# One score round moved behind the first MLP layer, and the words around it reordered, in a fused attention and MLP kernel

## The chip, the cores and the metric

The kernel runs on one core of one Trainium2 chip. The metric is the device time of one launch in microseconds (us); each kernel is timed in several runs and the median is compared. Five engines work side by side, each through its own instructions in order: TensorE (PE in the profile; its weight loads have a row of their own, PEld), VectorE (DVE), ScalarE (ACT), GpSimd (POOL) and SyncE (SP). SP and POOL also issue the DMA transfers. They wait for each other only through semaphores.

## The reference

Attention with a forget gate, followed by an MLP with a tanh GELU, over 8 batches of 576 tokens, 8 heads of 64 and a model width of 512. Cut to what matters:

```python
scores = scale * q @ k.T                                   # per batch and head, 576 x 576
cum = cumsum(log(clip(f, 1e-4, 1)))
scores = where(causal, -1e9, scores + cum[:, None] - cum[None, :])
attn = softmax(scores)
x = (attn @ v)            # -> (4608 tokens, 512)
h = x @ w_in              # 512 -> 2048
out = gelu_tanh(h) @ w_out  # 2048 -> 512
```

## The kernel before

The work is written out as a list of short words in tables (FRONT, SECOND, STEADY, FLUSH, LAST, lines 71 to 112). `run` (line 845) walks a table and emits the instructions of each word in that order; nothing is rescheduled afterwards, so the order of words is the order of instructions on every engine. FRONT covers everything up to the last pieces of chunk 1's second layer.

Attention is done by quads, a quad being four heads of one batch: quads 2 and 3 make batch 1, quads 4 and 5 batch 2, quad 6 begins batch 3. The MLP is done by chunks of 512 tokens. The words that matter here:

- `S.i.r` is score round r of quad i, `H.i.r.g` the same round for two of its four heads (`scores`, line 268). Matrix products of 32 rows, one for each head side by side, go into two PSUM tiles `ps_s` of two heads each (pool `psS`, two buffers); then ACT takes the exponential of each tile into `pt` (line 294), which frees the tile. A round of four heads takes both buffers, a half round one.
- `M.i.r` sets the entries above the diagonal to zero on POOL (line 300), `m.i.r` does it on DVE by a product with a triangle (line 330).
- `D.i` is the denominator product, one PSUM tile `po` and three DVE instructions (line 365); `V.i.x` and `v.i.x` are the two halves of the product with the values and their DVE division into `xT` (line 383). `v` uses a `psS` buffer in place of `po`.
- `VW.i` (POOL) and `vw.i` (DVE) weight the values into `vw` (line 234); `CL.i` (DVE) and `cl.i` (ACT) then copy one block of `vw` to other partitions (line 239). Two buffers each of `pt`, `vw`, `qT`, `kT`, `q_c`, `k_c` and `v_nat` alternate.
- `I.c.p` is one of eight pairs of the first layer of chunk c: eight products of 512 columns into a `psS` buffer, then a GELU on ACT (line 412).
- `F.c.n` and `f.c.n` emit n steps of the second layer of chunk c, in one matrix product of 128 columns of weights (`F`) or in four of 32 columns side by side (`f`). Chunk 0 has 64 steps (`mlp_out`, line 682), chunk 1 has 112 (`seven_products`, line 606).
- `J` is the first layer of chunk 0. `U`, `UW`, `PW` and `G` are sums of weights and of GELU results for the seven-product schemes, on DVE or POOL.
- `LK.i`, `LQ.i` load k and q of a quad from POOL's queue; `LV.b.half` loads four heads of v from SP's queue in five transfers; `LC` loads v from POOL's queue. `TK.i`, `TQ.i` transpose k and q on DVE.
- `X` and `Y` are one-element activations that touch the exponential and the GELU. ACT keeps the table of one of the two at a time; where the next function is of the other kind a table load stands before it.

Three places of the order matter for the steps below. In FRONT before, quad 4's round 0 is done in two halves, `H.4.0.0 H.4.0.1`, between `D.3` and `V.3.1`, ahead of the eight `I.1` words; `cl.4` stands behind all eight of them; and POOL issues `LK.5 LQ.6 LK.6` in a row, ahead of the masks `M.3.2` and of `VW.4`. `VW.4` reads the half of `v_nat` that `LV.2.0` loads.

Of the kernel before, what the change touches and what calls it, by code (L numbers as in the profile page):

```python
# [16 lines left out]
def kernel(  # L17
# [12 lines left out]
    B, H, S, D = q.shape  # L30
# [44 lines left out]
        H.1.0.0 B.1.128 B.1.512 B.1.128 B.1.512 M.1.0 B.1.128 V.0.1.0 H.1.2.0 H.0.1.1 V.0.0.0 H.0.3.0 D.1.0 V.1.1.0 j.0.0.4 M.0.1 UT LQ.2  # L75
        WI.7 V.1.0.0 H.0.3.1 H.1.3.1 j.0.0.4 j.0.0.8 H.1.1.0 vw.0.1 WI.6 H.1.1.1 RJ.0.0 M.0.3 D.0.1 LK.2 WO.1 WO.0 j.0.1.8 VW.1.1 H.1.2.1
        H.1.3.0 M.1.3 V.0.1.1 V.0.0.1 J.0.2 j.0.1.8 M.1.1 D.1.1 tr V.1.0.1 V.1.1.1 GJ.0.1 W.1 TQ.2 J.0.3 J.1.1 GJ.0.0 J.1.3 J.1.0 U.0 WO.2
        J.1.2 LK.3 WO.3 LQ.3 LC.1.0 PW.2.1 PW.2.2 F.0.3 LC.1.3 f.0.2 LC.1.4 LC.1.1 LC.1.2 TK.2 LQ.4 f.0.2 S.2.0 F.0.5 TK.3 m.2.0 F.0.4 LK.4
        F.0.1 S.2.2 F.0.2 f.0.5 TQ.3 f.0.2 S.2.1 f.0.3 LV.2.1 F.0.6 S.3.0 F.0.2 m.2.1 vw.2 cl.2 F.0.2 f.0.1 LV.2.0 X M.2.2 D.2 M.3.0 LQ.5
        f.0.1 S.3.1 VW.3 f.0.2 V.2.0 LK.5 TQ.4 TK.4 f.0.4 S.3.2 LV.3.1 LQ.6 f.0.1 m.3.1 f.0.3 LK.6 V.2.1 M.3.2 f.0.4 S.4.1 F.0.5 VW.4 TQ.5  # L80
        F.0.1 X H.4.2.0 H.4.2.1 D.3 f.0.1 cl.3 H.4.0.0 H.4.0.1 V.3.1 v.3.0 vw.5 U.1 f.0.2 m.4.2.2 I.1.2 I.1.1 UW.2.4 TK.6 I.1.0 CL.5 U.2
        m.4.2.3 I.1.3 I.1.5 TQ.6 U.3 TK.5 I.1.4 G.0 I.1.6 M.4.1 I.1.7 F.1.1 G.1.1.2 cl.4 F.1.5 LV.3.0 F.1.5 S.5.0 F.1.5 M.5.0 F.1.7 m.4.0
        F.1.2 UW.2.3 F.1.2 LK.8 F.1.7 LK.7 D.4 S.5.1 F.1.17 LQ.8 F.1.1 S.5.2 M.5.2.3 M.5.2.2 f.1.2 V.4.0 f.1.1 M.5.1 f.1.8 LQ.7@m.3.1 f.1.1
        V.4.1 S.6.0 M.6.0 f.1.4 D.5 f.1.10 S.6.1 f.1.1 M.6.1 f.1.2 V.5.1 vw.6 F.1.4 CL.6 F.1.5 S.6.2 m.6.2.3 V.5.0 f.1.4 m.6.2.2 f.1.3
    """

    SECOND = """
# [35 lines left out]
    def many(n, shape, dtype, name):  # L123
        return [singles.tile(shape, dtype, name=f"{name}{i}") for i in range(n)]
# [11 lines left out]
    vw = many(2, [128, NT + 1, 4, D], BF16, "vw")  # L136
# [760 lines left out]
```

## Time and profile before

| | |
|---|---|
| median of 3 runs | 320.56 us (320.35 to 320.78) |
| the profiled execution's own time | 320.43 us |
| its span, first to last instruction | 318.7 us |
| granted TensorE clock | 1.00 |
| first step of chunk 0's second layer starts | 38.4 us |
| quad 4's round 0 starts | 61.2 us |
| chunk 1's first layer | 64.3 to 78.1 us |
| chunk 2's first layer starts (FRONT is done) | 99.1 us |

All that the change touches lies between 38.4 and 99.1 us. The chain of waits names, in order of time, the work that the end hung on. A timeline lists the instructions of one engine with start and duration; what stands in brackets is the idle time before and who ended it. In both, "x24" counts instructions that are shown as one piece; some matmul records are missing, so the counts of matmuls can be a little low. In the chain a piece of matmuls lasts until the next piece starts.

### The profile page before, as it was taken

To read this page: it belongs to the slowest core of one execution; us is meant where nothing else is said; L and a number is where in the kernel's file an instruction comes from. 1 tells how busy PE (TensorE), PEld (TensorE's weight loads), DVE (VectorE), ACT (ScalarE), POOL (GpSimd) and SP (SyncE) were. 2 spreads that over 40 slices of the span, in tenths; PEclk is the share of its full clock that TensorE was granted. 3 is DMA by queue.
4 is the path that set the end of the run, shared out by engine and by line. 5 is a ranking of instruction groups with operands and counts; after the bars stand their busy time and mean duration, and the time that the engine had idled before them with its cause. 6 is when DMAs were issued, how large, how long until landed. Compare 5 with 4: busy or idle time off the path is not lost.

```text
span 318.7 us, 11738 instructions
## 1 busy us (share of the span) xinstructions
PE 313.0 (98%) x5290; PEld 220.3 (69%) x5309; DVE 246.0 (77%) x368; ACT 212.9 (67%) x248; POOL 109.6 (34%) x146
## 2 busy tenths in 40 slices
PE   8999999999999999999999999999999999999996
PEld 3468744545776577776788878767776786688785
DVE  7775638699978879879877987699876865597674
ACT  3676777866766876877777866787596744836610
POOL 8789525250340417311850075205610140000000
PEclk9999999999999999999999999999999999999999
DMA  7999998933364901593139411961011111010213
GB/s 126 239 203 199 209 227 190 233 106 75 70 117 127 193 6 39 129 199 72 39 80 232 89 39 37 217 147 38 5 39 62 35 37 35 30 38 2 99 35 100
DMA packets 47491, 33.41 MB, mean 105 GB/s; under 512 B 29777, under 2 KB 42193, under 8 KB 47441
## 3 DMA queue, kind: packets, MB, share of 16 engines
q0 software_dynamic: 9632, 15.99, 28.1%
q1 hardware_dynamic: 37664, 16.60, 19.4%
q8 instruction: 41, 0.67, 0.9%
q14 instruction: 10, 0.07, 0.1%
q10 hardware_dynamic: 144, 0.07, 0.1%
HBM read 36.85 MB, written 9.44 MB: 145 GB/s over the span
## 4 chain that ended last, share of the span: by engine, by line
PE 97%; issue 1%; DVE 0%; ACT 0%
PE ps_w L620 31%; PE ps_h L404 19%; PE ps_s L286 10%; PE ps_q L540 10%; PE po L356 9%; PE ps_h L440 5%; PE pso L693 4%; PE ps_u L488 4%; PE idle_ps L259 3%; PE po_m L342 2%; PE idle_ps L265 1%; PE ps_p L620 1%; PE ps_o L356 0%; ACT pt L294 0%; DVE xT L388 0%
## 5 line engine op out<-in xcount | busy, mean ns | idle before, releaser
L294 ACT ACTIVATE pt<-ps_s 128x1024 bf16<-128x1024 f32 (+2 forms) x100 | 93.9, 991 | 36.6 <-PE ps_s L286 34.9
L300 POOL TENSOR_SCALAR_AFFINE_SELECT pt<-pt 128x512 bf16<-128x512 bf16 (+3 forms) x70 | 44.3, 645 | 99.1 <-ACT pt L294 76.3
L404 PE MATMUL ps_h<-xT,w_in_sb 128*128 128x512 bf16 (+1 forms) x307 | 65.5, 357 | 0.8 <-issue 0.2
L404 PEld LDWEIGHTS <-w_in_sb 128*128 128x128 bf16 x320 | 31.1, 98 | 26.4 <-issue 0.6
L412 ACT ACTIVATE gT<-ps_h 128x1024 bf16<-128x1024 f32 x34 | 34.6, 1017 | 20.3 <-PE ps_h L404 20.1
L620 PEld LDWEIGHTS <-gT 128*32 128x32 bf16 (+1 forms) x1177 | 43.9, 97 | 5.7 <-issue 2.2
L620 PE MATMUL ps_w<-w_out_sb,gT 128*32 128x256 bf16 (+1 forms) x996 | 42.7, 273 | 0.0
L620 PEld LDWEIGHTS <-gsum 128*32 128x32 bf16 (+1 forms) x909 | 35.1, 97 | 3.9 <-issue 1.7
L286 PE MATMUL ps_s<-qT,kT 32*128 32x64 bf16 (+5 forms) x896 | 35.1, 261 | 0.1
L556 DVE TENSOR_TENSOR usnap<-ps_q,usnap 128x1024 f32<-128x1024 f32 x15 | 17.9, 1221 | 17.3 <-PE ps_q L540 12.7
L234 POOL TENSOR_TENSOR vw<-v_nat,wT 128x1280 bf16<-128x1280 f32 (+1 forms) x12 | 27.9, 2326 | 7.6 <-DMA v_nat<-in_v_dram 7.3
L620 PE MATMUL ps_w<-usum,gsum 128*32 128x256 bf16 (+1 forms) x752 | 29.8, 273 | 0.0
L286 PEld LDWEIGHTS <-kT 32*128 32x128 bf16 x896 | 16.1, 92 | 16.5 <-issue 10.8
L637 DVE COPY snap<-ps_w 128x512 f32<-128x512 f32 x32 | 21.8, 682 | 6.5 <-PE ps_w L620 6.3
L551 ACT ACTIVATE gT<-usnap 128x1024 bf16<-128x1024 f32 x15 | 15.8, 1053 | 11.0 <-DVE usnap L556 10.7
L388 DVE TENSOR_TENSOR xT<-po,rb 128x576 bf16<-128x576 f32 x26 | 19.5, 751 | 4.3 <-PE po L356 3.9
L356 PE MATMUL po<-pt,vw 128*32 128x64 bf16 (+4 forms) x624 | 22.4, 278 | 0.0
L217 DVE STREAM_TRANSPOSE kT<-k_c 128x576 f32<-128x576 f32 x16 | 19.4, 1244 | 2.5 <-DMA k_c<-in_k_dram 2.5
L356 PEld LDWEIGHTS <-vw 128*32 128x32 bf16 x672 | 14.6, 97 | 9.3 <-issue 2.6
L217 DVE STREAM_TRANSPOSE qT<-q_c 128x576 f32<-128x576 f32 x16 | 19.8, 1249 | 0.4 <-DMA q_c<-in_q_dram 0.3
L210 POOL DMA_DIRECT2D k_c<-in_k_dram x16 | 9.1, 570 | 30.0 <-DVE kT L217 17.4
L540 PEld LDWEIGHTS <-w_in_sb 128*128 128x128 bf16 x160 | 15.7, 98 | 2.1
(135 smaller groups left out, 491.7 us busy)
## 6 DMA issues: line engine op xcount, KB each, us to landing
out_dram<-o_st SPq DMA_DIRECT2D x35, 256.0 KB, 2.2
k_c<-in_k_dram POOLq DMA_DIRECT2D x16, 288.0 KB, 5.4
q_c<-in_q_dram POOLq DMA_DIRECT2D x16, 288.0 KB, 6.3
v_nat<-in_v_dram SPq DMA_DIRECT2D x16, 256.0 KB, 5.0
v_nat<-in_v_dram SPq DMA_DIRECT2D x20, 128.0 KB, 5.1
v_nat<-in_v_dram POOLq DMA_DIRECT2D x8, 256.0 KB, 9.6
w_in_sb<-in_moe_w_in_dram POOLq DMA_DIRECT2D x8, 256.0 KB, 8.5
w_out_sb<-in_moe_w_out_dram POOLq DMA_DIRECT2D x4, 512.0 KB, 11.3
```

Source lines behind the costliest of these rows:

```text
L217: return nc.vector.transpose(out=dst.rearrange("p s c -> p (s c)").bitcast(FP32) .rearrange("p (t a) -> p a t", a=n), in_=src.rearrange("p ...
L234: return eng.tensor_mul(vw[i % 2][:, t0:t1], vb[:, t0:t1, h0:h0 + 4, :], wT[:, i, t0:t1, :].unsqueeze(3).to_broadcast([128, t1 - t0, 4, D]))
L286: nc.tensor.matmul(tiles[h // 2][:, h % 2, c0:c0 + nq], key_columns(i, key, h, c), qq[32 * h:32 * h + 32, q0:q0 + nq, c], start=(c == 0 an ...
L294: nc.scalar.activation(p[:, 2 * g:2 * g + 2, off:off + n], t[:, :, 0:n], AF.Exp, scale=scale)
L300: nc.gpsimd.affine_select(out=x, in_=x, compare_op=ALU.is_ge, fill=0.0, base=0, pattern=pattern, channel_multiplier=-1)
L356: nc.tensor.matmul(po[r0:r0 + w.shape[-1], 448 + q0:448 + q0 + nq], w, p[:, h, col:col + nq], start=(key in (0, "low")), stop=(key in ("lo ...
L388: nc.vector.tensor_mul(xT[:, 2 * u + x, r0 + s0:r0 + s1], po, rbs[i, part])
L404: nc.tensor.matmul(ph[:, j, n * cols:(n + 1) * cols], w_in_sb[:, dt, 128 * ft:128 * ft + 128], xT[:, dt, h0:h0 + cols], start=(dt == 0 and ...
L412: nc.scalar.activation(gelus(c, 2 * pr, 2), ph, AF.Gelu_apprx_tanh)
L540: nc.tensor.matmul(ps[:, k, HC * n:HC * n + HC], w[:, d, 128 * n:128 * n + 128], x[:, d, :], start=(first and n == 0 and d == 0), stop=(d ...
L620: nc.tensor.matmul(ps[c0:c0 + width, n, cols[0]:cols[1]], x[:, j, 128 * n + c0:128 * n + c0 + width], w[:, j, cols[0]:cols[1]], start=(fir ...
L637: copy(kept[name], ps)
```

## The change

The tail of FRONT is rewritten, from the second layer of chunk 0 on. Other tables and all functions are as before.

```diff
-        J.1.2 LK.3 WO.3 LQ.3 LC.1.0 PW.2.1 PW.2.2 F.0.3 LC.1.3 f.0.2 LC.1.4 LC.1.1 LC.1.2 TK.2 LQ.4 f.0.2 S.2.0 F.0.5 TK.3 m.2.0 F.0.4 LK.4
-        F.0.1 S.2.2 F.0.2 f.0.5 TQ.3 f.0.2 S.2.1 f.0.3 LV.2.1 F.0.6 S.3.0 F.0.2 m.2.1 vw.2 cl.2 F.0.2 f.0.1 LV.2.0 X M.2.2 D.2 M.3.0 LQ.5
-        f.0.1 S.3.1 VW.3 f.0.2 V.2.0 LK.5 TQ.4 TK.4 f.0.4 S.3.2 LV.3.1 LQ.6 f.0.1 m.3.1 f.0.3 LK.6 V.2.1 M.3.2 f.0.4 S.4.1 F.0.5 VW.4 TQ.5
-        F.0.1 X H.4.2.0 H.4.2.1 D.3 f.0.1 cl.3 H.4.0.0 H.4.0.1 V.3.1 v.3.0 vw.5 U.1 f.0.2 m.4.2.2 I.1.2 I.1.1 UW.2.4 TK.6 I.1.0 CL.5 U.2
-        m.4.2.3 I.1.3 I.1.5 TQ.6 U.3 TK.5 I.1.4 G.0 I.1.6 M.4.1 I.1.7 F.1.1 G.1.1.2 cl.4 F.1.5 LV.3.0 F.1.5 S.5.0 F.1.5 M.5.0 F.1.7 m.4.0
-        F.1.2 UW.2.3 F.1.2 LK.8 F.1.7 LK.7 D.4 S.5.1 F.1.17 LQ.8 F.1.1 S.5.2 M.5.2.3 M.5.2.2 f.1.2 V.4.0 f.1.1 M.5.1 f.1.8 LQ.7@m.3.1 f.1.1
-        V.4.1 S.6.0 M.6.0 f.1.4 D.5 f.1.10 S.6.1 f.1.1 M.6.1 f.1.2 V.5.1 vw.6 F.1.4 CL.6 F.1.5 S.6.2 m.6.2.3 V.5.0 f.1.4 m.6.2.2 f.1.3
+        LK.3 WO.3 J.1.2 F.0.1 LQ.3 F.0.1 LC.1.0 PW.2.1 PW.2.2 F.0.3 LC.1.3 LC.1.4 LC.1.1 LC.1.2 TK.2 F.0.2 LK.4 S.2.0 LQ.4 F.0.5 TK.3 m.2.0
+        F.0.4 S.2.2 F.0.10 S.2.1 TQ.3 X F.0.3 LV.2.1 F.0.6 S.3.0 f.0.4 m.2.1 vw.2 cl.2 f.0.2 LV.2.0 M.2.2 D.2 M.3.0 LQ.5 S.3.1 VW.3 LV.3.1
+        f.0.4 LK.5 V.2.0 f.0.3 S.3.2 TK.4 f.0.2 TQ.4 V.2.1 M.3.2 m.3.1 f.0.5 S.4.1 LQ.6 f.0.2 LK.6 f.0.1 UW.2.4 f.0.2 D.3 f.0.1 VW.4 X cl.3
+        H.4.2.1 H.4.2.0 V.3.1 f.0.1 v.3.0 cl.4 F.0.2 I.1.7 I.1.0 TQ.5 TK.5 vw.5 cl.5 I.1.1 TK.6 TQ.6 I.1.2 I.1.5 U.1 I.1.4 I.1.3 U.2 F.1.1
+        m.4.2.2 I.1.6 LV.3.0 m.4.2.3 G.0 G.1.1.2 F.1.6 U.3 m.4.1 F.1.4 S.4.0 F.1.6 LK.8 F.1.6 m.4.0 F.1.2 S.5.0 M.5.0 PW.2.3 LK.7 D.4 f.1.9
+        S.5.1 F.1.12 LQ.8 F.1.6 S.5.2 M.5.2.2 M.5.2.3 V.4.0 f.1.2 m.5.1 f.1.4 f.1.5 V.4.1 S.6.0 M.6.0 f.1.6 D.5 f.1.6 S.6.1 M.6.1 f.1.5
+        V.5.1 f.1.5 vw.6 f.1.2 S.6.2 CL.6 m.6.2.3 f.1.4 M.6.2.2 V.5.0 LQ.7 f.1.6
```

What is other in kind, not only in place: `H.4.0.0 H.4.0.1` become `S.4.0`, behind the first layer and eleven second-layer steps of chunk 1; `CL.5` becomes `cl.5` (DVE to ACT); `M.4.1` and `M.5.1` become `m.4.1` and `m.5.1` (POOL to DVE), `m.6.2.2` becomes `M.6.2.2` (DVE to POOL), `UW.2.3` becomes `PW.2.3` (DVE to POOL). The steps of the second layers are the same in number, 64 of chunk 0 and 97 of chunk 1, divided otherwise between `F` and `f`: 31 and 33 of chunk 0 become 37 and 27, 61 and 36 of chunk 1 become 43 and 54. The extra dependency `@m.3.1` of `LQ.7` is gone. On ACT `cl.4` now stands ahead of the first GELU's table load, and POOL issues `LQ.6` and `LK.6` behind the two masks of `M.3.2`. SP's order of transfers is the same.

## The prediction, made before the changed kernel ran

> **What bounds the kernel.** I read the page's busy shares and the summary of the chain first.
>
> ```profile
> PE 313.0 (98%) x5290; PEld 220.3 (69%) x5309; DVE 246.0 (77%) x368; ACT 212.9 (67%) x248; POOL 109.6 (34%) x146
> PE 97%; issue 1%; DVE 0%; ACT 0%
> ```
>
> TensorE is busy 98% of the span and carries 97% of the chain. A change of order gains only by making TensorE's own stream cheaper, and loses whatever it lets TensorE wait. So I took the chain in order of time, from chunk 0's second layer to FRONT's end, for the price of each kind of piece:
>
> ```profile
> 42.91 0.57 PE ps_s L286 x14
> ...
> 60.21 0.80 PE po L356 x24
> 61.01 0.21 PE pso L693 x4
> 61.23 1.01 PE ps_s L286 x17
> ...
> 78.30 1.20 PE ps_w L620 x11
> 79.50 0.62 PE ps_s L286 x24
> 80.12 2.62 PE ps_w L620 x23
> 82.74 0.79 PE po L356 x24
> ...
> 87.08 0.68 PE po L356 x24
> 87.77 1.09 PE ps_w L620 x40
> ...
> 99.14 0.21 PE ps_h L404
> ```
>
> Eleven `F` steps of chunk 1 take 1.20 us (78.30), ten `f` steps, which are 40 products, 1.09 us (87.77): 0.109 us a step either way; a step of chunk 0 is 0.21 us (61.01). So `F` for `f` changes nothing in itself. But 23 `F` steps behind a score round take 2.62 us, where 23 x 0.109 is 2.51, and a product `po` behind `F` steps takes 0.79 (82.74), behind `f` steps 0.68 (87.08). Whenever TensorE changes between the three tilings (score rows; 128 columns: `F`, `I`, `J`; 32 columns: `f`, `D`, `V`) it loses 0.11 us, except on entering a score round: 11 steps and then scores (78.30) show no extra.
>
> **What the change gains.** Counting those changes of tiling in the two word lists, from the first step of chunk 0's second layer to the end of FRONT, I find 23 before and 17 after; 14 and 9 of them lie ahead of the `I.1` words. Six fewer: -0.66 us. Quad 4's round 0 in two halves takes 1.01 us (61.23), a whole round 0 takes 0.62 (79.50): -0.39. Two pieces of TensorE's timeline, the two halves of `H.4.2` and the eight `I.1` words:
>
> ```profile
> 58.84 1.38 PE L286 MATMUL ps_s<-qT,kT 32*128 32x320 bf16 x16
> ...
> 64.25 14.04 PE L404 MATMUL ps_h<-xT,w_in_sb 128*128 128x512 bf16 x62
> ```
>
> The halves start at 58.84 and `D.3` follows at 60.21, where two rounds of 0.57 (42.91) would be 1.14: about 0.25 is waiting, for the second exponential of `S.4.1` (57.60 + 1.94 in ACT's timeline below). After the change `D.3` stands between `S.4.1` and `H.4.2`, so that wait goes: -0.25. In sum -1.30 us.
>
> **What it loses on ACT and PSUM.** A round's tiles come free only with its exponentials, so the next whole round cannot finish its start before them. ACT's timeline:
>
> ```profile
> 40.76 1.94 ACT L294 ACTIVATE pt<-ps_s 128x1024 bf16<-128x1024 f32 x2
> ...
> 54.45 1.94 ACT L294 ACTIVATE pt<-ps_s 128x1024 bf16<-128x1024 f32 x2 [0.72 <-PE ps_s L286]
> ...
> 57.60 1.94 ACT L294 ACTIVATE pt<-ps_s 128x1024 bf16<-128x1024 f32 x2 [1.21 <-PE ps_s L286]
> ...
> 78.33 1.02 ACT L412 ACTIVATE gT<-ps_h 128x1024 bf16<-128x1024 f32 x1 [0.70 <-PE ps_h L404]
> 79.38 0.40 ACT L239 COPY vw<-vw 64x256 bf16<-64x256 bf16 x1
> 79.80 1.28 ACT L294 ACT_TABLE_LOAD   x1
> 81.10 1.94 ACT L294 ACTIVATE pt<-ps_s 128x1024 bf16<-128x1024 f32 x2
> ```
>
> Let T be the end of the last `I` (78.30 before). Before, the exponentials of `S.5.0` start late, at 81.10, behind GELU, copy and table load, but 23 steps and `D.4` stand before `S.5.1`, and that hides it. After: the GELU ends at T+1.05, with `cl.4` gone the load at T+2.35, the exponentials of `S.4.0` at T+4.31. TensorE needs ten steps (1.09), `S.4.0` (0.62), then 14 steps and a change of tiling (1.64): it is at `S.5.0` at T+3.35, and the heads of the second tile wait until T+4.35. That is +1.0 us. `S.5.1` follows behind `D.4` (0.79) and nine `f` steps (0.98), 1.77 us, where the exponentials of `S.5.0` need 1.94 and some 0.08 of handing over: +0.25. Later pairs of rounds have 2.0 us or more between them (18 `F` steps and a change of tiling are 2.07): nothing. At the front, `S.2.2` now comes after nine steps and no `f`, at about 42.6 instead of 42.91, while the exponentials of `S.2.0` still end at 42.70: +0.15. In sum +1.4 us; from below 1.0, if the two small ones are hidden, to 1.9, if `D.4` also waits. It waits for the mask `m.4.0`, now the last of a queue on DVE:
>
> ```profile
> 74.64 1.21 DVE L587 TENSOR_TENSOR w_out_sb<-w_out_sb 128x2048 bf16<-128x2048 bf16 x1
> ...
> 80.22 0.69 DVE L600 TENSOR_TENSOR gsum<-gsum,gT 128x1024 bf16<-128x1024 bf16 x1
> 80.83 0.68 DVE L637 COPY snap<-ps_w 128x512 f32<-128x512 f32 x1
> 81.43 0.41 DVE L330 TENSOR_TENSOR pt<-pt,causal 128x512 bf16<-128x512 bf16 x1
> ```
>
> From the GELU's end at T+1.1 on, two such sums (1.38), `U.3` (1.21), `m.4.1` (0.41), the copy (0.68) and `m.4.0` (0.41): T+5.2 without overlap, about T+5.0 with the tenth or so by which neighbours overlap in these rows; `S.5.0` ends at T+4.97. I take nothing for it.
>
> The Trainium skill (ScalarE: Activation LUTs, What ACT_TABLE_LOAD costs) speaks harder against the change: it states 1.28 us for the load and as much as 1.38 us of draining with every switch. The rows agree with the first and show no second: copy, load and exponential follow within 0.02 us. By the page's 2.66 us the wait at `S.5.0` alone would be 1.4 us longer.
>
> **What it loses behind `cl.4`.** `cl.4` copies what `VW.4` writes. Before, it stood behind all GELUs, and nobody noticed that `VW.4` ran late. Now table load and all GELUs of chunk 1 queue behind it, and TensorE waits for them with the third `I`, which needs the PSUM buffer of the first. POOL, SP and the transfers:
>
> ```profile
> 52.80 2.33 POOL L234 TENSOR_TENSOR vw<-v_nat,wT 128x1280 bf16<-128x1280 f32 x1
> 55.09 0.59 POOL L210 DMA_DIRECT2D k_c<-in_k_dram  x1
> 55.68 0.54 POOL L210 DMA_DIRECT2D q_c<-in_q_dram  x1
> 56.34 0.53 POOL L210 DMA_DIRECT2D k_c<-in_k_dram  x1
> 56.88 1.24 POOL L300 TENSOR_SCALAR_AFFINE_SELECT pt<-pt 128x512 bf16<-128x512 bf16 x2
> 65.39 2.90 POOL L234 TENSOR_TENSOR vw<-v_nat,wT 128x1280 bf16<-128x1280 f32 x1 [7.27 <-DMA v_nat<-in_v_dram]
> ```
>
> ```profile
> 55.06 2.37 SPq L187 DMA_DIRECT2D v_nat<-in_v_dram  x1
> ```
>
> ```profile
> k_c<-in_k_dram POOLq DMA_DIRECT2D x1, 288.0 KB, 6.7
> q_c<-in_q_dram POOLq DMA_DIRECT2D x1, 288.0 KB, 7.7
> k_c<-in_k_dram POOLq DMA_DIRECT2D x1, 288.0 KB, 8.7
> v_nat<-in_v_dram SPq DMA_DIRECT2D x1, 128.0 KB, 5.9
> v_nat<-in_v_dram SPq DMA_DIRECT2D x1, 64.0 KB, 10.2
> ```
>
> Added to their issue times, `LK.5` lands at 61.8, `LQ.6` at 63.4, `LK.6` at 65.0, and the last fifth of `LV.2.0`, whose issue took SP from 55.06 to 57.43, at 65.3; its neighbour one place ahead needed only 5.9. `VW.4` starts at 65.39 with that landing. The queue of v went almost silent while POOL's ran: the queue tables of the microseconds from 56 and from 60 have
>
> ```profile
> q1 hardware_dynamic: 941, 0.24, 105.4%
> ...
> q1 hardware_dynamic: 29, 0.01, 4.3%
> ```
>
> q1 being SP's queue. I read it as service in the order of arrival: the v piece came in behind all three loads of k and q.
>
> After the change the `I` words start at 64.25 less five changes of tiling (0.55), the moved round (1.01) and the wait (0.25), plus 0.15: 62.6. An `I` lasts 1.73 (eight products of 0.216, the 0.21 of a chunk 0 step), so the third starts at 66.05. Ahead of it ACT must do copy 0.40, load 1.28 and GELU 1.02, with hand-overs 2.8: `VW.4` must end by 63.25, and start by 60.9 at 2.33 us or 60.35 at 2.90. POOL now issues `LQ.6` and `LK.6` behind `M.3.2`, whose exponentials end at 56.39 before (54.45 + 1.94) and within 0.1 of that after: masks until 57.6, loads issued 57.6 and 58.2, just behind SP's 57.43. In order of arrival the v piece then waits only for `LK.5` (61.8) and lands 0.3 later (as 65.3 to 65.0): 62.1. `VW.4` ends 64.4 to 65.0, the GELU frees the buffer 67.2 to 67.8: +1.2 to +1.75, I take +1.5. Bounds: with its neighbour's 5.9 it lands at 61.0: +0.1; if nothing helps it, 65.3: +4.4 to +5.0. I take the value between since one of three loads stays ahead of it. It cannot be a gain.
>
> The other moved words I put at nothing. `cl.5` on ACT (0.40) falls into the 0.70 us that ACT idles before each GELU (78.33), and costs up to 0.4 there if `vw.5` is late; the masks moved to DVE have until `D.4` and `D.5`, and each costs its 0.41 if it is not ready; `PW.2.3` has POOL's idle time and until chunk 2 uses it; `LK.4` and `LQ.4` change places on POOL's queue, and the chain's summary, with 0% of DVE, shows nothing that waits for a transpose; `LQ.7` loses a gate, far from its use, and `LK.8` and `LK.7` stay behind the `I` words.
>
> **Sum.** -1.3 + 1.4 + 1.5 = +1.6 us on the profiled execution's 320.43: 322.0. The median is 0.13 above that execution, so 322.1 us.
>
> **Rivals.**
>
> *The load keeps its old place* (chance 0.20). A load issued only 0.2 us behind SP's last piece can still be served ahead of it, and then the v piece lands at 65.3: -1.3 + 1.4 + 4.7, 325.4 us. For it: the piece was slow although SP began to issue it at 55.06, ahead of `LK.5`; against it: its neighbour was not.
>
> *No wait behind `cl.4`* (0.22). The piece lands by 61, the gain and the waits on PSUM cancel: 320.7 us. For it, the 5.9 us of the neighbour; against it, `LK.5` landing at 61.8 on the same engines. The Trainium skill (DMA: Bandwidth & Descriptors, Queues, rings and completion order) states that each DMA engine takes turns between its queues packet by packet, and by that rule the time would be this one. The trace does not agree: 941 packets a microsecond against 29 are no turns at that scale.
>
> *Faster* (0.08). No wait behind `cl.4`, and `S.5.0` waits little, as the heads of the first tile run ahead: -1.3 + 0.3, 319.6 us. Against it: the products of the four heads are issued in turn, so the first of the second tile holds up the rest; it decides for this case only if the exponentials end by T+3.7.
>
> **Chances and range.** Forecast 0.50, the rivals 0.20, 0.22, 0.08. Within 0.2% (0.64 us, what a measurement of this kernel can tell from no change) is the third case; slower are the forecast and the first, 0.70. Low 320.2 and high 325.8 leave out the last case and the far sides of the first and third, 0.18 in all; the forecast's own range is 321.4 to 322.9.
>
> **What would show it.** Right: on ACT `cl.4` idle for POOL's `VW.4`, the first GELU of chunk 1 starting about 66 where TensorE finished its pair at 64.3, a hole of 1 to 2 us on TensorE in the third `I`, and another of 1 us at `S.5.0` behind a table load; `VW.4` starting near 62. Wrong: `VW.4` done by 63.2 with no hole in the `I` words; FRONT ending before 98.5; or a hole elsewhere, as at `D.4` or `D.3`.

## The result: slower by 0.56%

| | before | after |
|---|---|---|
| median | 320.53 us (8 runs, 320.35 to 322.08) | 322.50 us (8 runs, 321.51 to 323.15) |
| profiled execution | 320.43 us, span 318.7 | 321.97 us, span 320.0 |
| ratio of the times | | 1.0056, 95% interval 1.0044 to 1.0068 |

The loss is 1.97 us. The runs of after spread over 1.6 us, and its profiled execution is one of the faster ones: it shows 1.5 of the 2.0 us. Of these 1.5 the spans account for 1.3; time less span is 1.81 to 1.97 us in the eight runs of after and 1.7 in the kernel before, and no view shows what takes the 0.2 between them. One run among the experiments, 328.11 us in e6_early_loads, is more than 1.5% above the fastest of its kernel and is left out of the medians. Page of the profile after:

```profile
span 320.0 us, 11820 instructions
...
PE 314.0 (98%) x5345; PEld 221.3 (69%) x5345; DVE 244.1 (76%) x367; ACT 213.1 (67%) x249; POOL 108.5 (34%) x146
...
q8 instruction: 42, 0.69, 0.9%
...
PE 94%; ACT 2%; DVE 1%; DMA 1%; issue 0%
```

TensorE is still the bound, but ACT now has 2% of the chain, where before it had none. The chain of waits of after, in order of time:

```profile
42.63 0.81 PE ps_s L286 x10
...
62.65 12.14 PE ps_h L404 x56
...
76.67 1.02 ACT gT L412
77.71 1.28 ACT L294
79.00 1.95 ACT pt L294 x2
80.99 0.73 PE ps_s L286 x21
81.72 1.93 ACT pt L294 x2
83.69 0.63 PE ps_s L286 x14
...
99.58 1.73 PE ps_h L404 x8
```

From 76.67 on the chain runs through ACT: last GELU, table load, the exponentials of `S.4.0`, and only then the rest of `S.5.0`; one round later the exponentials of `S.5.0` hold up `S.5.1`. TensorE's timeline gives the sizes:

```profile
62.49 12.30 PE L404 MATMUL ps_h<-xT,w_in_sb 128*128 128x512 bf16 x56
...
80.08 0.20 PE L286 MATMUL ps_s<-qT,kT 32*128 32x64 bf16 x2
80.99 0.69 PE L286 MATMUL ps_s<-qT,kT 32*128 32x64 bf16 x22 [0.71 <-ACT pt L294]
81.61 0.87 PE L356 MATMUL po<-pt,w_bf 128*32 128x512 bf16 x24
...
83.39 0.94 PE L286 MATMUL ps_s<-qT,kT 32*128 32x64 bf16 x16
84.26 1.70 PE L620 MATMUL ps_w<-usum,gsum 128*128 128x256 bf16 x14
```

A timeline's duration runs a little into the next piece, so a round is best timed from its start to the start of what follows. `S.5.0` starts at 80.08 and `D.4` follows at 81.61: 1.53 us for a round 0, which takes 0.62 without waiting, so 0.91 us of waiting. `S.5.1` takes 0.87 (83.39 to 84.26) where 0.57 is usual, 0.30 too much; `S.2.2` takes 0.81 in the chain, 0.24 too much. The `I` words start at 62.49, where 64.25 stood before, and run through without a hole. Why there is none stands in the rows of POOL and ACT:

```profile
60.64 2.33 POOL L234 TENSOR_TENSOR vw<-v_nat,wT 128x1280 bf16<-128x1280 f32 x1 [1.54 <-DMA v_nat<-in_v_dram]
```

```profile
63.00 0.40 ACT L239 COPY vw<-vw 64x256 bf16<-64x256 bf16 x1 [0.89 <-POOL vw L234]
63.42 1.28 ACT L412 ACT_TABLE_LOAD   x1
64.72 1.02 ACT L412 ACTIVATE gT<-ps_h 128x1024 bf16<-128x1024 f32 x1
```

ACT does wait for `VW.4`, as predicted, but in this execution the v piece landed at 60.6. The first GELU ends at 65.74, and the third `I` is due at 62.49 + 2 x 1.73 = 65.95: 0.2 us to spare. FRONT ends at 99.58 against 99.14. The other 0.9 us of the span lie behind it: 0.6 in the last 4 us. DVE's last piece and the span's end are 2.89 us apart before (315.81 and 318.7), and 3.51 after:

```profile
316.49 0.29 DVE L660 TENSOR_TENSOR v_nat<-ps_p,snap 128x128 f32<-128x128 f32 x1 [0.15 <-PE ps_p L620]
```

### The profile page after: what moved, and what is told of

It is laid out like the page before. It is cut to its first block, busy times and chain, and to the rows that moved or that the text cites. A ratio compares the mean times of both kernels' runs of the same rounds, so it can differ in the third digit from the quotient of the medians.

```text
span 320.0 us, 11820 instructions
## 1 busy us (share of the span) xinstructions
PE 314.0 (98%) x5345; PEld 221.3 (69%) x5345; DVE 244.1 (76%) x367; ACT 213.1 (67%) x249; POOL 108.5 (34%) x146
## 4 chain that ended last, share of the span: by engine, by line
PE 94%; ACT 2%; DVE 1%; DMA 1%; issue 0%
PE ps_w L620 30%; PE ps_h L404 20%; PE ps_q L540 10%; PE ps_s L286 9%; PE po L356 9%; PE pso L693 5%; PE ps_h L440 5%; PE ps_u L488 4%; PE po_m L342 2%; ACT pt L294 1%; PE idle_ps L259 1%; DMA f_all<-in_f_dram 1%; PE idle_ps L265 1%; PE ps_p L620 1%; PE ps_o L356 0%; DVE f_all L729 0%
## 5 line engine op out<-in xcount | busy, mean ns | idle before, releaser
L300 POOL TENSOR_SCALAR_AFFINE_SELECT pt<-pt 128x512 bf16<-128x512 bf16 (+3 forms) x69 | 42.2, 623 | 105.0 <-ACT pt L294 82.2
L404 PE MATMUL ps_h<-xT,w_in_sb 128*128 128x512 bf16 (+1 forms) x320 | 67.0, 358 | 0.0
```

The source lines that it names most:

```text
L300: nc.gpsimd.affine_select(out=x, in_=x, compare_op=ALU.is_ge, fill=0.0, base=0, pattern=pattern, channel_multiplier=-1)
L404: nc.tensor.matmul(ph[:, j, n * cols:(n + 1) * cols], w_in_sb[:, dt, 128 * ft:128 * ft + 128], xT[:, dt, h0:h0 + cols], start=(dt == 0 and ...
```

## The experiments

Each kernel was timed beside the kernel before on the same chip; the last column is the difference of the two medians.

| | median (lowest to highest, runs) | less before |
|---|---|---|
| after | 322.50 (321.51 to 323.15, 8) | +1.97 |
| e1_cl4_late | 322.52 (321.49 to 324.73, 6) | +1.87 |
| e2_gap | 323.46 (322.32 to 324.37, 6) | +2.81 |
| e4_move | 323.25 (322.92 to 323.43, 5) | +2.76 |
| e5_regroup | 322.10 (321.99 to 322.96, 5) | +1.45 |
| e6_early_loads | 322.90 (322.63 to 326.77, 3) | +2.25 |
| e7_fewer_instructions | 322.00 (320.69 to 322.97, 12) | +1.51 |
| e8_regroup_same_count | 320.48 (320.20 to 320.79, 11) | -0.01 |
| e9_gap_masks | 322.39 (322.02 to 323.13, 5) | +1.90 |
| e10_cl4_late_short | 321.40 (321.13 to 321.99, 7) | +0.91 |
| e11_v_later | 322.51 (321.80 to 322.78, 5) | +2.02 |
| e12_all | 320.15 (320.00 to 320.83, 11) | -0.34 |
| e13_loads_behind | 322.27 (320.98 to 323.17, 6) | +1.61 |

### One part of the change alone, on the kernel before

**e4_move**, the moved round alone:

```diff
-cl.3 H.4.0.0 H.4.0.1 V.3.1
+cl.3 V.3.1
...
-F.1.5 S.5.0 F.1.5 M.5.0 F.1.7 m.4.0 F.1.2 UW.2.3 F.1.2 LK.8 F.1.7 LK.7 D.4 S.5.1
+F.1.5 S.4.0 F.1.5 F.1.7 m.4.0 F.1.2 S.5.0 M.5.0 UW.2.3 LK.8 LK.7 D.4 F.1.2 F.1.7 S.5.1
```

> The kernel before with one part of the change alone: H.4.0.0 H.4.0.1 go, S.4.0 stands behind the I.1 words and eleven steps, S.5.0 fourteen steps behind it, D.4 ahead of nine steps and S.5.1; the mask and load words in between keep their order. Theory A (prediction's terms): the halves' 1.01 us go or, since the I words then wait for DVE's xT, only part of them; 0.62 comes back, S.5.0 waits 1.3 us (cl.4 stands ahead of the table load here), S.5.1 0.3: +1.2 to +2.2, 321.8 to 322.8 us. Theory B (the waits for exponentials are hidden): 320.2 to 321.2.

Measured: +2.76 us, the direction of theory A, but 0.5 above its upper end. TensorE's timeline:

```profile
62.17 0.87 PE L356 MATMUL po<-pt,vw 128*32 128x512 bf16 x24 [0.68 <-DVE den L375]
...
82.23 0.20 PE L286 MATMUL ps_s<-qT,kT 32*128 32x64 bf16 x2 [0.41 <-ACT pt L294]
83.14 0.69 PE L286 MATMUL ps_s<-qT,kT 32*128 32x64 bf16 x22 [0.71 <-ACT pt L294]
```

The halves had covered DVE's work behind `D.3`. Without them `V.3.1` waits 0.68 us for it. The `I` words start at 64.08, against 64.25; but this execution was 0.27 us behind already at `D.3` (60.41 against 60.14), where the two kernels are still the same. From `D.3` to the `I` words it takes 3.67 us in place of 4.11, so 0.44 of the 1.01 us that the move takes away remain. The waits come in full: `S.5.0` waits 0.41 us and then 0.91 more than its 0.62 (82.23 to `D.4` at 83.76), where 1.3 was expected. The full change also puts `D.3` ahead of `H.4.2`, which then covers DVE's work.

**e5_regroup**, five changes of tiling fewer:

```diff
-F.0.3 LC.1.3 f.0.2 LC.1.4 LC.1.1 LC.1.2 TK.2 LQ.4 f.0.2 S.2.0
+F.0.3 LC.1.3 F.0.2 LC.1.4 LC.1.1 LC.1.2 TK.2 LQ.4 F.0.2 S.2.0
...
-S.2.2 F.0.2 f.0.5 TQ.3 f.0.2 S.2.1 f.0.3 LV.2.1 F.0.6 S.3.0 F.0.2 m.2.1 vw.2 cl.2 F.0.2 f.0.1
+S.2.2 F.0.2 F.0.5 TQ.3 F.0.2 S.2.1 F.0.3 LV.2.1 F.0.6 S.3.0 f.0.2 m.2.1 vw.2 cl.2 f.0.2 f.0.1
...
-V.5.1 vw.6 F.1.4 CL.6 F.1.5 S.6.2
+V.5.1 vw.6 f.1.4 CL.6 f.1.5 S.6.2
```

> The kernel before with one part of the change alone: nine words of second-layer steps change between F and f so that five changes of tiling go (four from the first chunk 0 step to S.3.0, one at S.6.2); no word is moved. Theory A (each change of tiling costs TensorE 0.11 us): 320.5 - 0.55 = 320.0 us. Theory B (the 0.11 us is hidden or is paid back in waits for exponentials, since the same rounds come closer together): 320.5 +-0.2.

Measured: +1.45 us; both theories miss. TensorE's timeline has the place, in the middle of `D.5`:

```profile
90.34 0.60 PE L356 MATMUL po<-pt,w_bf 128*32 128x512 bf16 x10
92.50 0.49 PE L356 MATMUL po<-pt,w_bf 128*1 128x448 bf16 x10 [1.56 <-issue]
```

Ten of 24 products are through, then TensorE stands for 1.56 us, and no semaphore released it ("issue"). The queue tables of this kernel from 88 to 90 and from 90 to 92 us (packets, MB, share of 16 engines):

```profile
q0 software_dynamic: 190, 0.40, 107.9%
...
q8 instruction: 1, 0.02, 3.0%
```

q0 is POOL's queue with loads of k and q; q8 brings TensorE's instructions in blocks of 0.69 MB / 42 = 16.4 KB. The table from 88 to 90 has no q8 row: the block came only then, behind the loads. In the kernel before, the transfers of q8 near this place lie between 84 and 86 and between 90 and 92. By `D.5` ten steps net have become `F`, a product and a weight load each in place of four and four: 60 instructions fewer, so the boundary of a block falls on another place.

**e8_regroup_same_count** tests that: the last swap of e5 is left out, and ten steps in a gap between two rounds become `f`, which changes no tiling and gives the 60 instructions back:

```diff
-S.2.0 F.0.5 TK.3 m.2.0 F.0.4 LK.4 F.0.1 S.2.2
+S.2.0 f.0.5 TK.3 m.2.0 f.0.4 LK.4 f.0.1 S.2.2
```

> e5_regroup without its last swap, and the ten steps between S.2.0 and S.2.2 as f in place of F, which changes no tiling but gives back the 60 TensorE instructions that e5 saves: four changes of tiling fewer than the kernel before, and every instruction behind D.2 at its old place in the stream. Theory A (e5 lost 1.9 us because a block of instructions began elsewhere and its transfer came behind loads of k and q; a change of tiling is worth 0.11 us): no idle TensorE at D.5, 320.6 - 0.44 = 320.1 to 320.3 us. Theory B (the loss of e5 comes from the regrouping itself, through DVE or ACT): 321.5 to 322.5.

Measured: -0.01 us, far from theory B and 0.2 above theory A. The idle time at `D.5` is gone, so it hung on the count of instructions ahead of it; that the block was late because of the loads is read from the queue tables. The gain of four changes of tiling does not show in the median (ratio 0.9995, interval 0.9987 to 1.0004: 0.2 us could hide in it). Its chain:

```profile
43.36 0.58 PE ps_s L286 x16
...
45.99 0.65 PE ps_s L286 x16
...
48.77 0.63 PE ps_s L286 x20
...
50.59 0.68 PE po L356 x24
```

From `S.2.2` (43.36) to `S.2.1` (45.99) are 2.63 us, where before has 2.72 (42.91 to 45.63), and from `S.3.0` to `D.2` 1.82, where it has 1.92: 0.1 each as predicted. From `S.2.1` to `S.3.0` it is 2.78 against 2.74: `S.2.1` arrives earlier and takes 0.65 in place of 0.57. There the change of tiling saved ahead of the round is lost; that the round then waits for exponentials fits these rows, but no row names the wait.

### Where after loses

**e1_cl4_late** and **e10_cl4_late_short** take `cl.4` out of the GELUs' way, e10 on top of e7:

```diff
-v.3.0 cl.4 F.0.2 I.1.7 ... I.1.2 I.1.5
+v.3.0 F.0.2 I.1.7 ... I.1.2 cl.4 I.1.5
```

> The changed kernel with cl.4 taken from ahead of the I.1 words to behind the third of them, so that neither the GELU table load nor a GELU of chunk 1 waits for VW.4; nothing else is moved. Theory A (the prediction's term: VW.4's data lands late in most runs and holds up the GELUs, although the profiled run of after escaped with about 0.2 us to spare): the median falls from 322.5 us by 0.5 to 1.5, to 321.0-322.0, and the spread of the runs (321.5 to 323.2) narrows. Theory B (cl.4 costs nothing, as in that profile): 322.4 +-0.2, with the same spread; the table load starts about 2 us earlier and nothing comes of it.

Measured for e1: +1.87 us, 322.52, which is theory B: no gain over after. Its six runs spread over 3.2 us, too much to see 0.5 in. The profiled one, the slowest, had lost 1.1 us already in the first 10 us, where a score round waited for a transpose of q; no `I` word waits in it, although `VW.4` starts only at 64.13. **e7_fewer_instructions** first takes the tail away:

```diff
-V.5.0 LQ.7 f.1.6
+V.5.0 LQ.7 F.1.6
```

> The changed kernel with its last word f.1.6 written F.1.6: the same six steps in one product each in place of four, 18 products and 18 weight loads fewer, at the same number of changes of tiling, and all of it behind what the prediction speaks of. The page of after counts 42 instruction transfers of 16 KB on q8 where the kernel before has 41; the 42nd falls into the last 5 us, and the stretch from DVE's last piece to the end is 3.5 us there, against 2.9. Theory A (one block of TensorE instructions more, fetched at the very end, delays the end): back to 41 transfers, that stretch back to 2.9 us, 322.5 - 0.6 = 321.9 us. Theory B (the tail is an accident of the profiled run): 322.5 +-0.2.

Measured: +1.51 us, 0.46 less than after: theory A. The page counts 41 transfers on q8, and the end is back at 2.87 us behind DVE's last piece (318.23, span 321.1). The runs of the two kernels overlap, but the profiles agree: that end takes 3.51, 3.73 and 3.88 us in the three kernels with 42 transfers (after, e1, e6), and 2.87 to 2.95 in the eleven with 41. And e7's profiled execution, its slowest, shows what the profile of after did not. Its chain of waits:

```profile
54.61 8.14 DMA v_nat<-in_v_dram
...
62.91 2.35 POOL vw L234
65.28 0.40 ACT vw L239
65.70 1.28 ACT L412
67.00 1.03 ACT gT L412
68.07 8.79 PE ps_h L404 x40
```

and TensorE's waits (what waited for what: us in total, times, longest):

```profile
PE ps_h L404 <- ACT gT L412: 1.4, 1, 1.4
...
PE pso L693 <- issue: 0.6, 1, 0.6
```

The v piece landed at 62.75, and v, POOL, copy, table load and GELU in a row set the third `I`, which waited 1.35 us: the predicted chain, link by link. So the two executions differ in when one transfer landed.

> e7_fewer_instructions with cl.4 behind the third I.1 word, as in e1_cl4_late. In e7's profile VW.4's data came at 62.8 us, and TensorE stood 1.35 us ahead of the third I; in the profile of after it came at 60.6 and nothing was lost: two executions, two outcomes. Theory A (the wait behind cl.4 comes and goes with the landing of v, and is part of most executions): the median falls below e7's 322.0 us by 0.4 to 1.0, to 321.0-321.6, and the slowest runs with it. Theory B (the runs differ by something else, such as TensorE's instructions coming late behind the same loads, 0.60 us of idle time in e7 and 1.12 in e9 ahead of the f step behind V.3.1): 321.8 to 322.2.

Measured: +0.91 us, 0.60 less than e7, and 0.9 us of spread in place of 2.3: theory A. POOL's and TensorE's rows in its profile:

```profile
63.20 2.33 POOL L234 TENSOR_TENSOR vw<-v_nat,wT 128x1280 bf16<-128x1280 f32 x1 [3.75 <-PE pso L693]
```

```profile
62.90 12.31 PE L404 MATMUL ps_h<-xT,w_in_sb 128*128 128x512 bf16 x56
```

The piece was issued at 55.8, took 7.2 us and landed at 63.0, later than in e7 (the bracket names PE, whose products ended last before it), and yet the `I` words run through: with `cl.4` out of the way a late piece costs nothing there. With `cl.4` ahead of the `I` words, the third `I` waits in five of seven profiles, 0.82 to 1.46 us (e6, e7, e9, e11, e13; not in those of after and e2). What this is worth over many runs is known only roughly: e10's runs lie within the range of e7's, and e1, the same move on after, shows no gain.

**e6_early_loads** puts the two loads back ahead of the masks on after:

```diff
-V.2.1 M.3.2 m.3.1 f.0.5 S.4.1 LQ.6 f.0.2 LK.6 f.0.1
+V.2.1 LQ.6 LK.6 M.3.2 m.3.1 f.0.5 S.4.1 f.0.2 f.0.1
```

> The changed kernel with LQ.6 and LK.6 put back ahead of the masks M.3.2 on POOL, as they stood before; nothing else. Theory A (service in order of arrival: loads of k and q that POOL issues before SP's last piece of v is through hold that piece up): the piece lands at 64 to 65.5 instead of 60.6, VW.4 and cl.4 run 4 us later and the third I waits 3.5 to 4.5 us: 325.5 to 327 us. Theory B (the queues share the DMA engines evenly): the piece lands within 1.5 us of 60.6, at most 1.5 us is lost: 322.5 to 324.

One run took 326.8 us, as theory A has it, and two took 322.6 and 322.9, as theory B has it; the run left out took 328.1. In the profiled run, at 322.9, the piece landed at 61.9 and the third `I` waited 0.89 us, so with more loads ahead of it the piece need not come later. That it came 4 us later in the long runs fits their time, but no profile shows it.

**e13_loads_behind** asks which load it is, on e7:

```diff
-S.4.1 LQ.6 f.0.2 LK.6 f.0.1 UW.2.4 f.0.2 D.3 f.0.1 VW.4 X
+S.4.1 f.0.2 f.0.1 UW.2.4 f.0.2 D.3 f.0.1 VW.4 LQ.6 LK.6 X
...
-cl.5 I.1.1 TK.6 TQ.6 I.1.2
+cl.5 I.1.1 I.1.2
...
-LV.3.0 m.4.2.3 G.0
+LV.3.0 m.4.2.3 TK.6 TQ.6 G.0
```

> e7_fewer_instructions with LQ.6 and LK.6 issued by POOL behind VW.4 (their transposes on DVE moved behind the triangle masks, so that nothing waits for them); cl.4 stays ahead of the I.1 words. LK.5 is then the only load of k and q issued between 54 us and VW.4. Theory A (LQ.6 and LK.6, issued at 58.0 and 58.6 us, pass the last v piece, which SP issued at about 54.6): the piece lands by 60.6, no idle TensorE at the third I, 320.7 to 321.2 us. Theory B (the prediction's choice: LK.5, issued at 55.1, is what the piece waits for, the two behind it do not matter): it still lands at 62 to 63 in most executions, 321.7 to 322.3 us.

Measured: +1.61 us, no different from e7: theory B. POOL's rows and, from the table of DMA issues, `LK.5`:

```profile
55.34 0.59 POOL L210 DMA_DIRECT2D k_c<-in_k_dram  x1
...
62.05 2.33 POOL L234 TENSOR_TENSOR vw<-v_nat,wT 128x1280 bf16<-128x1280 f32 x1 [3.75 <-DMA v_nat<-in_v_dram]
64.33 0.59 POOL L210 DMA_DIRECT2D q_c<-in_q_dram  x1
```

```profile
k_c<-in_k_dram POOLq DMA_DIRECT2D x1, 288.0 KB, 6.4
```

`LK.5` lands at 55.34 + 6.4 = 61.7 and the v piece at 61.9, with no other load of POOL on its way. In e7 the two are 62.4 (54.99 + 7.4) and 62.75.

**e11_v_later** takes another load out of the crowd:

```diff
-S.3.1 VW.3 LV.3.1
+S.3.1 VW.3
...
-v.3.0 cl.4 F.0.2 I.1.7
+v.3.0 LV.3.1 cl.4 F.0.2 I.1.7
```

> e7_fewer_instructions with the load LV.3.1 (five transfers, 576 KB, not needed before chunk 2) taken from behind LV.2.0 on SP's queue to behind the product v.3.0, about 62 us; cl.4 stays ahead of the I.1 words. So the DMA engines carry less between 54 and 62 us, where both the v piece of VW.4 and a block of TensorE's instructions come late in some executions. Theory A (both are late because of the crowd of transfers there): no idle TensorE behind V.3.1 and at the third I, the median falls to 320.7-321.2, near the fastest run of e7 (320.69), and the spread shrinks. Theory B (what holds them up is POOL's loads of k and q alone): 321.6 to 322.3.

Measured: +2.02 us, no gain, 0.2 above theory B's range. The v piece landed at 62.5 in its profile, just behind `LK.5` (55.20 + 7.0 = 62.2), and held up the third `I` by 1.46 us, as theory B has it. No run moves `LK.5` itself: that the piece waits for it is read from the landings in e7, e11 and e13. The idle TensorE behind `V.3.1` is absent there, but one execution does not settle that.

**e2_gap** and **e9_gap_masks** lengthen the gap ahead of `S.5.0`; here e9, with e7's edit in it too:

```diff
-F.1.6 LK.8 F.1.6 m.4.0 F.1.2 S.5.0 M.5.0 PW.2.3 LK.7 D.4 f.1.9 S.5.1 F.1.12 LQ.8
+F.1.6 LK.8 F.1.6 m.4.0 F.1.9 S.5.0 M.5.0 PW.2.3 LK.7 D.4 f.1.12 S.5.1 F.1.8 LQ.8
...
-f.1.4 f.1.5 V.4.1 S.6.0 M.6.0 f.1.6 D.5 f.1.6 S.6.1
+f.1.4 f.1.2 V.4.1 S.6.0 M.6.0 f.1.4 D.5 f.1.5 S.6.1
```

> The changed kernel with nine more F steps between S.4.0 and S.5.0 (23 in place of 14) and three more f steps ahead of S.5.1 (12 in place of 9), taken from the gaps behind, which keep more than the 2.0 us that a round's exponentials need; the work is the same. Theory A (S.5.0 and S.5.1 wait on TensorE for exponentials, 0.96 and 0.37 us in the profiled run of after): both waits go, 322.5 - 1.3 = 321.2 us; some 0.1 more or less for changes of tiling. Theory B (the loss of after lies elsewhere: behind cl.4, in the tail, in instruction fetches): less than 0.4 us is gained, 322.1 or more.

e2 had 23 steps there, `F.1.6 LK.8 F.1.15 m.4.0 F.1.2`, with the steps taken from the same gaps and from the last word, and lost 0.84 us more than after: theory B. Its waits:

```profile
PE po L356 <- DVE pt L330: 1.3, 1, 1.3
...
PE ps_w L620 <- DVE snap L637: 0.4, 1, 0.4
```

The wait for ACT is gone from the list, but the steps that moved forward brought their DVE work with them (`snap`, and the sums of the first corner) ahead of the mask `m.4.0`, and `D.4` now waits 1.31 us for it.

> As e7, and the gaps of e2_gap made so that D.4 need not wait: seven F steps more between S.4.0 and S.5.0, with m.4.0 issued ahead of them so that DVE has the mask before the sums of the first corner, and three f steps more ahead of S.5.1; ten fewer in the gaps behind. Theory A (S.5.0 and S.5.1 wait 0.96 and 0.37 us for exponentials): 1.0 to 1.3 us less than e7, 320.6 to 320.9 if e7 is at 321.9. Theory B (the waits only move on to the next product that needs a late engine, as in e2_gap): less than 0.4 us below e7.

Measured: +1.90 us, not below e7: theory B. `D.4` no longer waits, yet the rounds in TensorE's timeline still do:

```profile
83.37 0.92 PE L286 MATMUL ps_s<-qT,kT 32*128 32x64 bf16 x24
...
88.53 1.08 PE L286 MATMUL ps_s<-qT,kT 32*128 32x320 bf16 x16
...
94.48 0.95 PE L286 MATMUL ps_s<-qT,kT 32*128 32x64 bf16 x16
```

`S.5.0` takes 0.92 in place of 0.69, and `S.5.2` and `S.6.1`, from whose gaps the steps were taken, take 1.08 and 0.95 in place of 0.64 each (durations in the timeline, of rounds that do not wait): the waits have moved on. This execution also lost 1.25 us at the third `I` and 1.12 behind `V.3.1`, places that are as in e7.

**e12_all** puts the parts together, with the steps taken from behind `S.5.2`:

```diff
-F.0.4 S.2.2 F.0.10 S.2.1
+F.0.5 S.2.2 F.0.9 S.2.1
...
-S.3.1 VW.3 LV.3.1
+S.3.1 VW.3
...
-v.3.0 cl.4 F.0.2 I.1.7 ... I.1.2 I.1.5
+v.3.0 LV.3.1 F.0.2 I.1.7 ... I.1.2 cl.4 I.1.5
...
-m.4.0 F.1.2 S.5.0 M.5.0 PW.2.3 LK.7 D.4 f.1.9
+m.4.0 F.1.9 S.5.0 M.5.0 PW.2.3 LK.7 D.4 f.1.12
...
-f.1.4 f.1.5 V.4.1 S.6.0 M.6.0 f.1.6 D.5
+f.1.4 f.1.2 V.4.1 S.6.0 M.6.0 f.1.4 D.5
...
-vw.6 f.1.2 S.6.2 CL.6 m.6.2.3 f.1.4 M.6.2.2 V.5.0 LQ.7 f.1.6
+vw.6 f.1.1 S.6.2 CL.6 m.6.2.3 f.1.4 M.6.2.2 V.5.0 LQ.7 F.1.2
```

> All parts together on the changed kernel: cl.4 behind the third I.1 word, LV.3.1 behind v.3.0, the last f.1.6 as F, seven F steps more ahead of S.5.0 and three f more ahead of S.5.1 (taken behind S.5.2, not between S.5.1 and S.5.2 as in e9, where ACT then held up S.5.2 and S.6.1), one step more ahead of S.2.2. Theory A (after's loss is these five things): e11's time less 0.8 to 1.3 us for the waits for exponentials, 319.6 to 320.3, faster than both kernels. Theory B (ACT has no slack left in that stretch, the waits move on): 320.5 to 321.2.

Measured: -0.34 us, ratio 0.9991 with an interval of 0.9982 to 1.0000: theory A, the fastest of all kernels here, if only just faster than before. Its spans are 0.7 us shorter than before's (318.1 against 318.8 in the median), while its time less span is 0.3 us longer, 2.0 against 1.7. Its chain no longer goes through ACT in this stretch:

```profile
77.78 0.71 PE ps_s L286 x23
78.49 2.40 PE ps_w L620 x21
81.05 0.69 PE ps_s L286 x20
81.75 0.80 PE po L356 x24
```

## Why the prediction was right, and where it was not

Forecast 322.1, measured 322.5, inside the forecast's own range. The medians give an account of the 1.97 us: -0.34 is what is left of the gain once the losses are taken out (e12); +1.25 are mainly the waits for exponentials (e10 less e12, in which `LV.3.1` moves too and TensorE has 18 instructions fewer); +0.60 the wait behind `cl.4` (e7 less e10); +0.46 the end (after less e7). Only the step from e10 to e12 is clear of the spread of the runs (321.13 at the lowest, 320.83 at the highest); the sizes of the two smaller ones are uncertain. That the sum comes so close is in part luck: the gain is 1.0 us smaller than predicted and the wait behind `cl.4` 0.9, which cancel, and the end was not in the sum.

- **The waits on ACT and PSUM, +1.4: right, in place and size.** The profile has 0.91 + 0.30 + 0.24 = 1.45 for `S.5.0`, `S.5.1` and `S.2.2`, where 1.0, 0.25 and 0.15 were predicted; `D.4` does not wait, and e12 against e10 gives 1.25.
- **The wait behind `cl.4`, +1.5: right mechanism, too large on average.** The signs named are all in e7's profile, `VW.4` at 62.91, the GELU at 67.00, 1.35 us at the third `I`; e13 has 62.05 and 66.13, where 62 and 66 were predicted. That the piece lands just behind `LK.5` holds in e7, e11 and e13, by 0.2 to 0.4 us. What was mis-sized is its share: the landing differs from execution to execution, 60.6 in the profile of after and 62.75 in e7's, and over the runs the term is worth some 0.6 us. Order of arrival alone does not decide the landing: with the same order of issue the piece came ahead of `LK.5` in after and behind it in e7.
- **The gain, -1.3: too large.** The `I` words start at 62.49, predicted 62.6, but not quite by the terms of the sum. For `H.4.2` the prediction priced each half, of 8 products, at a whole round's 0.57, and so read 0.25 us of waiting. After, the two halves take 0.74 us (to `V.3.1` at 60.25) in place of 1.30 (58.84 to 60.14), 0.56 less (row below). Against that, e8 shows three of four changes of tiling paying 0.1 us each in its profile and none in the median, e4 shows that the moved round by itself brings 0.44 of its 1.01 us, and e12 keeps 0.34 us of time, or 0.7 of span.

```profile
59.51 0.69 PE L286 MATMUL ps_s<-qT,kT 32*128 32x320 bf16 x16
```

- **What was missing, +0.46.** The sentence that fails is "So `F` for `f` changes nothing in itself". It is true of TensorE's time a step; but an `f` step is four products and four weight loads, and 36 products more on balance gave TensorE's stream a 42nd block, fetched in the last 5 us. The prediction counted products, tilings and waits, not instructions.
- **The rivals.** "No wait behind `cl.4`" describes the profiled execution, not the median. Against it the prediction set 941 packets and 29 of one queue at two times; side by side, in the microsecond from 60 of before, POOL's queue moved 98 packets and SP's 29, which are no equal turns either. "The load keeps its old place" did not happen in after; with the loads put back, e6 has long runs of 326.8 and 328.1 us, for 325.4 predicted, which no profile shows. The condition of "faster" (exponentials done by T + 3.7) failed: they ended at 80.94, with T at 76.5.

Four things stay open: why the v piece was ahead of `LK.5` in the profile of after; how much of the loss and spread of after is late instruction blocks (0.60 us behind `V.3.1` in e7, 1.12 in e9, none in after; some 0.3 at `V.5.1` in after, where weight loads break off for 0.25 us with no releaser: only the case of e5 was tested); 0.27 us that after loses at 228 us, far behind the change; and the 0.2 us outside the span.

## What to carry to other kernels

Where the bound engine's words are regrouped, count its instructions too: a change of a few dozen moves the block boundaries behind it, and a block that comes due while loads fill the DMA engines can stop the engine, 1.56 us in e5. A gap made longer ahead of one waiting round is taken from another: find out first where the slower engine, here ACT with 1.94 us a round, has slack, and which engine's work the moved steps bring along. And one profiled execution can miss a wait that most executions have: where something hangs on a transfer's landing with 0.2 us to spare, take several.

## What was not expected of the hardware

TensorE can run out of instructions in the middle of a tile, with 1.56 us of idle time in e5 and nothing in the profile to name it but "issue" and a q8 row. The Trainium skill (Runtime: NRT & Kernel Launch, Instruction fetch mechanics) says that instructions are streamed in blocks of 16 KiB, 256 instructions, over a queue of the engine's own, and calls the cost mostly hidden. The size agrees: 42 transfers for 2 x 5345 products and weight loads. In before no idle time of TensorE under "issue" is longer than 0.2 us; in e5 one is 1.56, and there the cost was not hidden.

Two transfers on different queues, issued within 0.5 us of each other, landed in either order: the v piece of SP at 60.6 or 62.75 us, `LK.5` of POOL at 61.5 or 62.4, in kernels whose queues are the same up to there.
